# Moving work on VectorE's queue in a fused recurrence and gated-MLP kernel: C scaling earlier and chained, chunk 2's statistics in phase 0, norms one a group, two y slots within phase 3

## The chip, the cores and the metric

The kernel runs on one NeuronCore of a Trainium2 chip. The metric is the device time of one execution in microseconds (us). Most executions agree within about 1%. Each kernel was run several times beside the kernel before, on the same chip. "Span" is the length of the profiled execution as the profile sees it, some 2 us less than its time. The engines are PE (TensorE matmul; PEld in a page is its weight load), DVE (VectorE), ACT (ScalarE), POOL (GpSimd) and SP (here the queue that issues most DMAs).

## The reference, cut to what matters

```python
x = A_x                                   # 1 x 2048 x 448, bf16
xn = layernorm(x)
# A: a diagonal complex recurrence over the 2048 tokens
Lam_bar = exp(dt * (Lambda_re + 1j * Lambda_im))
B_bar = ((Lam_bar - 1) / Lam)[:, None] * (B_re + 1j * B_im)
h[t] = Lam_bar * h[t-1] + B_bar @ xn[t]
s = 2 * real(h @ C.T) + xn * Dskip
# B: a gated MLP, F = 1792
g = silu((sigmoid(xn @ w_gate) * (xn @ w_up)) @ w_down)
out = x + s * g
```

## The kernel before

The 2048 tokens are cut into four chunks of 512, and the program into four phases. In phase c, PE computes gate, up and B products of chunk c ("gu" banks), the down product of chunk c-1 ("acc") and y of chunk c-2 ("acc"). ACT evicts gu and computes sigmoids. DVE multiplies gate and up into hF, runs the recurrence (ta, tb, z, two scans "wv", then hT) and finishes the outputs. Before a chunk can be multiplied it is normalized: DVE takes its statistics, POOL a power, ACT writes xn, and a DMA transposes xn to xnT.

Every engine executes its own instructions in program order. A small planner at build time decides DVE's order: `side` is a queue of recurrence and similar steps, `late` holds evictions with an estimated time.

```python
def stat(g, t0, i, n):                    # one token tile of 128: mean and variance
    V.bn_stats(out=stats[:], in_=x_all[:, t0 + i, :])
    V.bn_aggr(out=mvs[g][:, i, :], in_=stats[:])
def stat_chain(g, t0, n, ...):            # -mean and, through POOL's power, 1/sd
    ...
    nc.gpsimd.tensor_tensor(out=sd_b, in0=ve_b, in1=half[:], op=ALU.pow)
    ...
def norm_slot(tt):                        # a tile of chunks 2 and 3
    xm = norm_a(tt, False); norm_b(tt, xm, False)    # ACT
    dup(tt)                               # POOL
    dma_transpose(tt)                     # SP queue

def c_steps():                            # C scaled by a per-state constant: 8 items
    def scaled(i): nc.scalar.activation(tmps[i][r, :], re, ACT.Copy, scale=...)   # ACT half
    def go(i): V.scalar_tensor_tensor(out=dst, in0=im, ..., in1=tmps[i][r, :], ...)  # DVE half -> cT
    ...
def ssm(c):                               # chunk c's recurrence into DVE's side queue
    ss = ssm_steps(c)                     # pair(0) + pair(1) + stack() + pair(2)
    if c == 0:                            # woven in, one after each step from the ninth on:
        ex = []
        for g in (2, 3):                  # statistics of chunks 2 and 3
            ex += [(0.7, lambda i=i, g=g: stat(g, 4 * g, i, 4)) for i in range(4)]
            ex.append((0.4, lambda g=g: stat_chain(g, 4 * g, 4)))
        ex.append((0.6, emit_diag))
        ss = weave(ss, ex + c_steps(), 8, 1)         # then the C items
    side.extend(ss)

def y_slot(c, j):                         # PE: xnT x diag(Dskip) + hT x cT
    ...
    for i, (hm, cm) in enumerate(K_ORDER):
        nc.tensor.matmul(y[:, cols], lhsT=hTs[c][:, hm, ...], rhs=K["cT"][:, cm, cols], ...)
# ... cut
run_phase(layout(2, "gbg gbg gbg gbg ggg ggg"), sides, norms(3, 0, 4))   # first y slots: chunk 0
ssm(3)
d, y = downs(2), ys(1)
sides = [[y[k], d[k]] for k in range(4)] + [[], []]
run_phase(layout(3, "gbg gbg gbg gbg ggg ggg"), sides)
for dur, fn in ys(2) + downs(3) + ys(3):
    plan.slot(dur, fn)
```

## Time and profile before

| | before |
|---|---|
| time, median of the first 3 runs | 205.41 us (205.40 to 206.59) |
| span of the profiled execution | 202.7 us |
| PE, DVE, ACT busy | 93%, 86%, 58% |
| PE idle for cT in the first y of chunk 0 | 3.8 us |

The page of the profile, parts 1, 2 and 4: busy time of each engine, then busy tenths of PE and DVE and the clock granted to PE in 40 slices of 5.07 us, and the shares of the chain of waits by engine.

```profile
PE 188.7 (93%) x1032; PEld 86.6 (43%) x1047; DVE 173.6 (86%) x385; ACT 116.6 (58%) x214; POOL 15.5 (8%) x38
...
PE   7999999899999999966999999999999999789983
...
DVE  7979895589999669963389999999999999999964
...
PEclk9999999999999999996999999999999999999999
...
DVE 47%; PE 6%; ACT 3%; issue 1%
```

PE is busy nearly everywhere from the second slice on. Two slices (86 to 96 us) read 6, and PEclk reads 6 in the second of them and 9 in its neighbours. The chain of work that ended last runs through DVE for 47% of the span.

What PE waited for (columns: engine, line, what the wait ended on; then us in total, times, longest):

```profile
PE acc L721 <- DVE cT L448: 3.8, 2, 2.4
PE acc L718 <- DVE g_t L725: 1.7, 2, 1.5
...
PE acc L721 <- DVE hT L632: 1.0, 1, 1.0
```

The timeline of PE at the first y (start, duration, engine, line, operation, out<-in, shapes, count; in brackets the idle time before it and its releaser):

```profile
87.77 0.36 PE L718 MATMUL acc<-diag,xnT 128*128 128x128 bf16 x4
87.97 1.11 PE L721 MATMUL acc<-cT,hT 128*128 128x448 bf16 x5
90.45 0.35 PE L721 MATMUL acc<-cT,hT 128*128 128x448 bf16 x1 [1.37 <-DVE cT L448]
93.22 0.53 PE L721 MATMUL acc<-cT,hT 128*128 128x448 bf16 x1 [2.42 <-DVE cT L448]
93.54 2.82 PE L697 MATMUL acc<-wd,hFa 128*128 128x448 bf16 x7
96.16 1.66 PE L697 MATMUL acc<-wd,hFb 128*128 128x448 bf16 x7
97.65 0.81 PE L470 MATMUL gu<-xnT,wg 128*128 128x512 bf16 x3
```

One y slot takes 1.52 us when nothing stops it, one down slot 2.65. Here y lasts from 87.77 to 93.54, and the down slot behind it from 93.54 to 97.65, because the clock fell. That is 9.88 us instead of 4.17.

The timeline of DVE: the first z of chunk 0, the first of chunk 2's statistics, the last hT of chunk 0, the last C item, and the first step of chunk 1's recurrence.

```profile
41.09 0.69 DVE L606 TENSOR_TENSOR z<-ta,tb 128x1024 bf16<-128x1024 bf16 x1
...
50.91 0.62 DVE L234 BATCH_NORM_STATS2 stats<-x_all 128x6 f32<-128x448 bf16 x1
...
86.55 0.72 DVE L632 TENSOR_TENSOR hT<-ta_1194,tb_1198 128x1024 bf16<-128x1024 bf16 x1
...
92.48 0.68 DVE L448 SCALAR_TENSOR_TENSOR cT<-cw,n2r,ctmp 64x448 bf16<-64x448 bf16 x1 [1.37 <-ACT ctmp L443]
...
99.16 0.69 DVE L592 TENSOR_TENSOR ta<-bus,cosT 128x1024 bf16<-128x1024 bf16 x1
```

### The profile page before, as it was taken

How to read it: one execution, taken by the hardware profiler on the slowest of the kernel's cores; microseconds unless marked ns; L12 is line 12 of the kernel's file. 1: busy time of each engine (PE TensorE's matmuls, PEld its weight loads, DVE VectorE, ACT ScalarE, POOL GpSimd, SP SyncE). 2: the span in 40 equal slices, each digit the busy share in tenths (PEclk: the TensorE clock that was granted, in tenths of full speed). 3: DMA queues.
4: the chain of work that ended last, by engine and by line, in shares of the span. 5: the costliest groups of instructions: out<-in, count | busy, mean ns of one | idle time of the engine just before them, and what ended most of it. 6: DMA issues, size and time to landing. Idle time of an engine off the chain costs nothing.

```text
span 202.7 us, 2922 instructions
## 1 busy us (share of the span) xinstructions
PE 188.7 (93%) x1032; PEld 86.6 (43%) x1047; DVE 173.6 (86%) x385; ACT 116.6 (58%) x214; POOL 15.5 (8%) x38
## 2 busy tenths in 40 slices
PE   7999999899999999966999999999999999789983
PEld 2564343244444443322454444354544443445542
DVE  7979895589999669963389999999999999999964
ACT  2539689895357999992375851654462836403300
POOL 4502302000030400000000000000000000000000
PEclk9999999999999999996999999999999999999999
DMA  5899998400000220011001010000000000011002
GB/s 165 267 326 156 261 358 173 82 0 0 0 0 3 52 52 0 2 29 49 0 0 49 27 26 23 0 0 26 0 24 0 26 23 0 0 49 45 0 23 70
DMA packets 23238, 12.08 MB, mean 60 GB/s; under 512 B 14772, under 2 KB 23224, under 8 KB 23224
## 3 DMA queue, kind: packets, MB, share of 16 engines
q1 hardware_dynamic: 22928, 11.73, 23.0%
q10 hardware_dynamic: 296, 0.18, 0.3%
q8 instruction: 8, 0.13, 0.3%
q14 instruction: 6, 0.05, 0.1%
HBM read 6.66 MB, written 1.84 MB: 42 GB/s over the span
## 4 chain that ended last, share of the span: by engine, by line
DVE 47%; PE 6%; ACT 3%; issue 1%
DVE wv L612 11%; DVE g_t L725 4%; DVE hT L632 3%; DVE z L606 3%; DVE x_all L726 3%; DVE tb L592 2%; DVE ta L592 2%; DVE hFb L520 2%; PE acc L697 2%; PE acc L721 2%; DVE hFa L520 2%; DVE g_t L705 2%; PE gu L470 1%; ACT ctmp L443 1%; ACT ub L514 1%
## 5 line engine op out<-in xcount | busy, mean ns | idle before, releaser
L470 PE MATMUL gu<-xnT,wg 128*128 128x512 bf16 (+1 forms) x168 | 44.8, 369 | 2.1 <-issue 1.1
L470 PE MATMUL gu<-xnT,wu 128*128 128x512 bf16 (+1 forms) x173 | 45.0, 368 | 0.4
L513 ACT ACTIVATE sig<-gu 128x512 bf16<-128x512 f32 x43 | 26.4, 614 | 22.3 <-PE gu L475 22.2
L700 ACT ACTIVATE sigd<-acc 128x448 bf16<-128x448 f32 x16 | 8.7, 542 | 38.9 <-PE acc L697 38.8
L721 PE MATMUL acc<-cT,hT 128*128 128x448 bf16 (+1 forms) x112 | 23.8, 348 | 4.8 <-DVE cT L448 3.8
L470 PEld LDWEIGHTS <-wg 128*128 128x128 bf16 x177 | 15.2, 97 | 25.4 <-issue 12.4
L514 ACT CAST ub<-gu 128x512 bf16<-128x512 f32 x43 | 25.8, 600 | 0.0
L470 PEld LDWEIGHTS <-wu 128*128 128x128 bf16 x177 | 17.3, 98 | 19.0
L697 PE MATMUL acc<-wd,hFa 128*128 128x448 bf16 x112 | 25.1, 366 | 0.1
L697 PE MATMUL acc<-wd,hFb 128*128 128x448 bf16 x112 | 24.0, 354 | 0.0
L475 PE MATMUL gu<-xnT,wk 64*128 64x512 bf16 (+1 forms) x118 | 18.9, 369 | 0.1
L697 PEld LDWEIGHTS <-hFa 128*128 128x128 bf16 x112 | 11.3, 100 | 13.9 <-issue 4.0
L470 PE MATMUL gu<-xnT,bT 128*128 128x512 bf16 x70 | 17.1, 379 | 0.0
L697 PEld LDWEIGHTS <-hFb 128*128 128x128 bf16 x112 | 11.1, 99 | 10.6 <-issue 0.7
L721 PEld LDWEIGHTS <-hT 128*128 128x128 bf16 x119 | 10.4, 98 | 9.7 <-issue 1.6
L552 ACT CAST bus<-gu 128x1024 bf16<-128x1024 f32 x12 | 12.4, 1030 | 0.8 <-PE gu L475 0.8
L520 DVE TENSOR_TENSOR hFb<-sig,ub 128x512 bf16<-128x512 bf16 x22 | 8.9, 417 | 3.5 <-ACT ub L514 3.5
L725 DVE TENSOR_TENSOR g_t<-acc,g_t 128x448 bf16<-128x448 f32 (+1 forms) x16 | 9.7, 603 | 2.1 <-PE acc L721 2.1
L520 DVE TENSOR_TENSOR hFa<-sig,ub 128x512 bf16<-128x512 bf16 x21 | 8.6, 412 | 3.1 <-ACT ub L514 3.1
L509 ACT ACTIVATE th<-gu 128x512 f32<-128x512 f32 x13 | 8.0, 614 | 5.1 <-PE gu L475 5.0
L470 PEld LDWEIGHTS <-bT 128*128 128x128 bf16 x72 | 7.0, 98 | 8.5
L475 PEld LDWEIGHTS <-wk 64*128 64x128 bf16 x118 | 5.0, 94 | 12.4 <-issue 9.7
(211 smaller groups left out, 270.7 us busy)
## 6 DMA issues: line engine op xcount, KB each, us to landing
out_dram<-x_all SPq DMA_DIRECT2D x15, 112.0 KB, 1.7
wd<-in_B_w_down_dram SPq DMA_DIRECT2D x1, 1568.0 KB, 9.0
wg<-in_B_w_gate_dram SPq DMA_DIRECT2D x2, 480.0 KB, 7.7
wu<-in_B_w_up_dram SPq DMA_DIRECT2D x2, 480.0 KB, 8.4
x_all<-in_A_x_dram SPq DMA_DIRECT2D x1, 896.0 KB, 5.4
x_all<-in_A_x_dram SPq DMA_DIRECT2D x1, 448.0 KB, 6.3
wg<-in_B_w_gate_dram SPq DMA_DIRECT2D x1, 384.0 KB, 4.3
wu<-in_B_w_up_dram SPq DMA_DIRECT2D x1, 384.0 KB, 4.1
```

The costliest lines, as they stand in the source:

```text
L470: nc.tensor.matmul(self.bank[:, i, cols], lhsT=get(kt), rhs=self.xnT[:, kt, cols], start=(kt == 0 and first), stop=(kt == KF - 1 and not f ...
L475: nc.tensor.matmul(self.bank[:, i, cols], lhsT=ap, rhs=self.xnT[r, 3, cols], start=first, stop=not first)
L513: nc.scalar.activation(th[:], gu[:, 0, :], ACT.Sigmoid)
L514: nc.scalar.copy(out=ub[:], in_=gu[:, 1, :])
L520: V.tensor_tensor(out=hF, in0=th[:], in1=ub[:], op=ALU.mult)
L552: nc.scalar.copy(out=bus[:], in_=bu[:])
L592: V.tensor_tensor(out=t[dst][:], in0=src, in1=tab, op=ALU.mult)
L612: V.tensor_tensor_scan(out=t["wv"][:, k, :], data0=rb, data1=t["z"][:, k, :], initial=(st[pt][:, k, :] if c else 0.0), op0=ALU.mult, op1=A ...
L697: nc.tensor.matmul(dacc[:, 0:D], lhsT=hF_at(c, ft)[:, j * P:(j + 1) * P], rhs=wd[:, ft, :], start=(ft == 0), stop=(ft == FT - 1))
L700: nc.scalar.activation(sigd[:], dacc[:, 0:D], ACT.Sigmoid)
L721: nc.tensor.matmul(y[:, cols], lhsT=hTs[c][:, hm, j * P:(j + 1) * P], rhs=K["cT"][:, cm, cols], start=False, stop=(i == 6))
L725: V.tensor_tensor(out=g_t[:, cols], in0=y[:, cols], in1=g_t[:, cols], op=ALU.mult)
```

## The change

Four edits move work; none removes or adds any. (1) The C items start right after the first pair of chunk 0's recurrence, and each item puts the next but one in motion, as "late" work, instead of standing in the weave. (2) Chunk 2's statistics leave the weave and go into phase 0. (3) `run_phase` gives out one norm a group instead of all that are ready. (4) Two of chunk 2's four y slots go between the last gate groups of phase 3.

```diff
@@ c_steps
-        steps = [(0.0, lambda i=i: scaled(i)) for i in range(2)]
-        for i in range(n):
-            if i + 2 < n:
-                steps.append((0.0, lambda i=i: scaled(i + 2)))
-            steps.append((0.6, lambda i=i: go(i), lambda i=i: scaled_at[i]))
-        return steps + [(0.0, lambda: h_done.add("c"))]
+        def step(i):
+            go(i)
+            if i + 2 < n:
+                start(i + 2)
+            if i == n - 1:
+                h_done.add("c")
+        def start(i):
+            scaled(i)
+            plan.add_late(scaled_at[i], 0.6, lambda: step(i))
+        return [(0.0, lambda: (start(0), start(1)))]
@@ phase 0, ahead of the edge constants
     side += [(0.7, lambda i=i: V_norm(4 + i), ...) for i in range(4)]
+    side += [(0.7, lambda i=i: stat(2, 8, i, 4)) for i in range(4)]
+    side.append((0.4, lambda: stat_chain(2, 8, 4)))
     side.append((0.0, constants))
@@ ssm
-            ex = []
-            for g in (2, 3):
-                ex += [(0.7, lambda i=i, g=g: stat(g, 4 * g, i, 4)) for i in range(4)]
-                ex.append((0.4, lambda g=g: stat_chain(g, 4 * g, 4)))
-            ex.append((0.6, emit_diag))
-            ss = weave(ss, ex + c_steps(), 8, 1)
+            ex = c_steps() + [(0.6, emit_diag)]
+            ex += [(0.7, lambda i=i: stat(3, 12, i, 4)) for i in range(4)]
+            ex.append((0.4, lambda: stat_chain(3, 12, 4)))
+            ss = weave(ss, ex, 8, 1)
@@ run_phase
-            while extras and extras[0][0] <= p and (p == len(groups) - 1 or ...):
+            last = p == len(groups) - 1
+            n = len(extras) if last else 1 + (bool(extras) and p > extras[0][0] + 1)
+            while n and extras and extras[0][0] <= p and (last or ...):
                 extras.pop(0)[1]()
+                n -= 1
@@ phase 3
-    sides = [[y[k], d[k]] for k in range(4)] + [[], []]
+    z = ys(2)
+    sides = [[y[k], d[k]] for k in range(4)] + [[z[0]], [z[1]]]
     run_phase(layout(3, "gbg gbg gbg gbg ggg ggg"), sides)
-    for dur, fn in ys(2) + downs(3) + ys(3):
+    for dur, fn in z[2:] + downs(3) + ys(3):
```

More of the change, by code (lines that the diff above doesn't have):

```diff
@@ L843, in run_phase @@
             group(units)
-            while extras and extras[0][0] <= p and (p == len(groups) - 1 or not extras[0][2] or extras[0][2]()):
+            last = p == len(groups) - 1
+            n = len(extras) if last else 1 + (bool(extras) and p > extras[0][0] + 1)
+            while n and extras and extras[0][0] <= p and (last or not extras[0][2] or extras[0][2]()):
                 extras.pop(0)[1]()
+                n -= 1
             for dur, fn in (sides[p] if sides else ()):
```

## The prediction

> **What bounds it now.** The span is 202.7 us; PE is busy 93% of it, DVE 86% (page, part 1). From 8 us on PE runs its stream back to back; time is lost where it stops. The inner stops (timeline and waits of PE): 0.94 us at 38.5 us; 1.37 and 2.42 us in the first y of chunk 0 (88 to 93 us), released by DVE writing cT; 1.49 and 0.21 us before y of chunk 2 (acc not freed by DVE's g_t); 1.00 us in y of chunk 3, for the last hT. The long stop also costs clock: from 91 to 96 us 0.6 is granted, and the next down slot takes 4.1 us instead of 2.65. The Trainium skill ("TensorE: Matmul & The Clock Gate", Part 1) says that about one idle window of 3.4 us halves the clock; the trace agrees: 3.8 us idle in two pieces, then starts 0.37 us apart instead of 0.19.
> From 94 us the chain of waits runs through DVE, filled to the end (52.1 of 53 us from 140 us): a backlog, since chunk 1's recurrence begins only at 99.2 us, behind C scaling, statistics and waits (2.34 us for rsd, 1.1 and 1.5 for ub, 1.4 for ctmp, 4.0 for g_t).
>
> **What the change does.** Work is only moved.
> - The eight C items (0.60 us each on DVE, 0.57 on ACT), now at 75 to 93 us, follow the first pair of chunk 0's recurrence, from about 50 us; cT should be complete by 65 us. C lies in memory by 36 us.
> - Chunk 2's statistics (3.1 us of DVE, at 51 to 57 us) go into phase 0, where DVE idles 1.3 + 1.2 + 2.2 us from 33 to 41 us; their x landed by 26 us. The edge constants slip; the first recurrence at most 1 us.
> - Norms one a group: ACT no longer holds four in a row (64.9 to 70.1 us), POOL's power for chunk 3's rsd isn't stuck behind four copies; the 2.34 us wait goes.
> - Two of chunk 2's y slots go between the last gate groups, so their evictions spread.
>
> **On the critical path.** Chunk 0's hT, finished at 87.3 us, should be done by 81 to 84 (3.1 us of statistics and 3 to 4 us of idle less, 1.8 us of C more). PE reaches y of chunk 0 at 87.8 us and won't stop: 3.8 + 1.45 us. DVE then runs over 10 us ahead; chunk 3 is held only by y of chunk 1, so its hT is ready: 1.0 us. Of the 1.7 us before y of chunk 2 I count 1.0. Sum 7.2 us, less 0.2 for new collisions: 7 us. PE's stream is the floor; over 8.5 us can't come out.
>
> **Prediction:** 198.4 us, 196.8 to 201.0. Faster by over 2%: 0.90, within 2%: 0.09, slower: 0.01.
>
> **What would show it.** Waits: no "PE acc <- DVE cT"; "acc <- DVE hT" under 0.3 us; "acc <- DVE g_t" under 1 us. Clock 0.9 or more in every slice from 10 us on. Timeline of DVE: cT written from 50 to 65 us; chunk 1's first ta before 86 us. The chain of waits mostly PE in the second half. DVE and ACT busy times change by under 2 us.
>
> **What would make it wrong.** Phase 0 slips: statistics delay the edge constants, tanh is kept longer (0.60 instead of 0.33 us on DVE an item), PE stops over 1 us around 39 us. ACT in phase 1, with norms and C halves, frees the gu banks late. DVE, gated by y of chunk 1, puts gate products behind a recurrence, so that PE waits for gu or hF. Then 201 us or more.

## The result, and the profile after

The changed kernel takes 196.99 us (median of 4 runs, 196.42 to 198.03), the kernel before beside it 205.91 us (4 runs). The ratio is 0.957, with a 95% interval from 0.9514 to 0.9627. Ratios here are the mean time of one kernel's fast runs over that of the other's fast runs of the same rounds, so not quite the ratio of the quoted medians. The results are correct.

The page after, the same parts:

```profile
PE 189.8 (97%) x1047; PEld 87.0 (44%) x1047; DVE 174.0 (89%) x385; ACT 116.4 (59%) x214; POOL 16.9 (9%) x38
...
PE   7999999998999999999999999999999999999992
...
DVE  7739989945999999999999999999999399999964
...
PEclk9999999999999999999999999999999999999998
...
PE 90%; ACT 3%; DMA 2%; issue 1%; DVE 1%; ACTq 1%; POOL 0%
```

PE reads 9 in every slice but one from the second to the last but one, the clock never falls before the end, and the chain that ended last is now PE for 90%. What PE waited for, all of it (the first is the warm-up at the start):

```profile
PE wps L222 <- POOL one L160: 1.3, 1, 1.3
PE gu L477 <- ACT ub L521: 0.8, 1, 0.8
PE gu L477 <- ACT ub L517: 0.2, 1, 0.2
PE gu L477 <- DVE xnT L293: 0.2, 1, 0.2
```

The three waits shown of before are gone. One of 0.84 us, for a gu bank at 46.75 us, is there instead. PE at the first y:

```profile
89.91 0.36 PE L725 MATMUL acc<-diag,xnT 128*128 128x128 bf16 x4
90.10 1.49 PE L728 MATMUL acc<-cT,hT 128*128 128x448 bf16 x7
91.43 1.49 PE L704 MATMUL acc<-wd,hFa 128*128 128x448 bf16 x7
92.75 1.49 PE L704 MATMUL acc<-wd,hFb 128*128 128x448 bf16 x7
94.08 0.81 PE L477 MATMUL gu<-xnT,wg 128*128 128x512 bf16 x3
```

The stretch that took 9.88 us takes 4.17. DVE after, the same instructions (the last hT of chunk 0 is at 87.69), and the last hT of chunk 3 (186.41).

```profile
35.31 0.62 DVE L234 BATCH_NORM_STATS2 stats<-x_all 128x6 f32<-128x448 bf16 x1
...
51.65 0.69 DVE L613 TENSOR_TENSOR z<-ta,tb 128x1024 bf16<-128x1024 bf16 x1
...
77.84 0.68 DVE L448 SCALAR_TENSOR_TENSOR cT<-cw,n2r,ctmp 64x448 bf16<-64x448 bf16 x1
...
87.69 0.69 DVE L639 TENSOR_TENSOR hT<-ta,tb 128x1024 bf16<-128x1024 bf16 x1
88.29 0.69 DVE L599 TENSOR_TENSOR ta<-bus,cosT 128x1024 bf16<-128x1024 bf16 x1
```
```profile
186.41 0.69 DVE L639 TENSOR_TENSOR hT<-ta,tb 128x1024 bf16<-128x1024 bf16 x1
```

**Start and body.** The start differs from run to run: the first gate matmul begins at 8.37 us in the profiled execution before and at 10.98 us in the one after, which was the slowest of its four. The columns after must be read 2.6 us earlier when they are compared. I call "body" the span minus the start of the first gate matmul. It is a steadier measure of one trace than the span: 194.33 us before and 185.02 after. A second profile of the changed kernel (after_again, below) gave 185.46. Cut at the same places of PE's stream:

| stretch of PE's stream | before, us | after, us | gained |
|---|---|---|---|
| first gate matmul to the first of phase 1 | 31.03 | 30.02 | 1.01 |
| to the first y of chunk 0 | 48.37 | 48.91 | -0.54 |
| that y and the down slot behind it | 9.88 | 4.17 | 5.71 |
| to the first y of chunk 3 | 94.07 | 92.07 | 2.00 |
| to the very last y part | 6.52 | 5.40 | 1.12 |
| to the end | 4.46 | 4.45 | 0.01 |
| body | 194.33 | 185.02 | 9.31 |

The first two rows differ between executions of one kernel: in after_again they are 31.48 and 47.90 us (PE stops there 1.38 us ahead of phase 1, and not later), together 0.02 us less than before. The three rows below them repeat; they sum up to 8.83 us.

### The profile page after: what moved, and what is told of

It reads as the page before. It is cut to its first block, busy times and chain, and to the rows that moved or that the text cites. A ratio compares the mean times of both kernels' runs of the same rounds, so it can differ in the third digit from the quotient of the medians.

```text
span 196.0 us, 2932 instructions
## 1 busy us (share of the span) xinstructions
PE 189.8 (97%) x1047; PEld 87.0 (44%) x1047; DVE 174.0 (89%) x385; ACT 116.4 (59%) x214; POOL 16.9 (9%) x38
## 4 chain that ended last, share of the span: by engine, by line
PE 90%; ACT 3%; DMA 2%; issue 1%; DVE 1%; ACTq 1%; POOL 0%
PE gu L477 45%; PE acc L704 22%; PE acc L728 10%; PE gu L482 9%; PE wps L222 2%; DMA vrow<-in_A_Lambda_im_dram 2%; PE acc L725 2%; ACT L520 1%; DVE g_t L732 1%; ACT th L516 1%; PE tpx L288 1%; ACT ub L517 1%; DVE x_all L733 0%; PE tpx L290 0%; ACTq L208 0%
## 5 line engine op out<-in xcount | busy, mean ns | idle before, releaser
L477 PE MATMUL gu<-xnT,wg 128*128 128x512 bf16 (+1 forms) x177 | 46.2, 370 | 1.2 <-ACT ub L521 0.8
L477 PE MATMUL gu<-xnT,wu 128*128 128x512 bf16 (+1 forms) x177 | 45.9, 368 | 0.0
L520 ACT ACTIVATE sig<-gu 128x512 bf16<-128x512 f32 x42 | 25.8, 614 | 22.5 <-PE gu L482 22.4
L521 ACT CAST ub<-gu 128x512 bf16<-128x512 f32 x42 | 25.2, 600 | 0.0
L704 PE MATMUL acc<-wd,hFa 128*128 128x448 bf16 x112 | 23.8, 352 | 0.0
L728 PE MATMUL acc<-cT,hT 128*128 128x448 bf16 (+1 forms) x112 | 23.2, 347 | 0.0
L619 DVE TENSOR_TENSOR_SCAN wv<-r_col,st,z 128x512 bf16<-128x512 f32 x18 | 22.6, 1276 | 0.2
L282 POOL COPY xn<-xn 128x64 bf16<-128x64 bf16 x12 | 6.5, 538 | 73.4 <-ACT xn L278 63.3
L516 ACT ACTIVATE th<-gu 128x512 f32<-128x512 f32 x14 | 8.6, 614 | 5.1 <-PE gu L482 5.0
```

The costliest lines, as they stand in the source:

```text
L477: nc.tensor.matmul(self.bank[:, i, cols], lhsT=get(kt), rhs=self.xnT[:, kt, cols], start=(kt == 0 and first), stop=(kt == KF - 1 and not f ...
L516: nc.scalar.activation(th[:], gu[:, 0, :], ACT.Tanh, scale=0.5)
L520: nc.scalar.activation(th[:], gu[:, 0, :], ACT.Sigmoid)
L521: nc.scalar.copy(out=ub[:], in_=gu[:, 1, :])
L619: V.tensor_tensor_scan(out=t["wv"][:, k, :], data0=rb, data1=t["z"][:, k, :], initial=(st[pt][:, k, :] if c else 0.0), op0=ALU.mult, op1=A ...
L704: nc.tensor.matmul(dacc[:, 0:D], lhsT=hF_at(c, ft)[:, j * P:(j + 1) * P], rhs=wd[:, ft, :], start=(ft == 0), stop=(ft == FT - 1))
```

## The experiments

**Theory.** PE's stream is the floor, and the change is worth exactly the stops that it takes out of this stream. **Rivals.** DVE's backlog is the bound (the chain before says so), so what counts is the DVE time moved. And, as to the four parts: each pays its own share, or only some of them matter.

| kernel | median, us | ratio to before, 95% | body, us |
|---|---|---|---|
| changed kernel | 196.99 | 0.957 (0.9514 to 0.9627) | 185.02 |
| c_alone: before + part 1 | 201.24 | 0.973 (0.9641 to 0.982) | 188.45 |
| stats_alone: before + part 2 | 197.27 | 0.9583 (0.9519 to 0.9647) | 185.19 |
| no_c: changed - part 1 | 196.80 | 0.956 (0.949 to 0.9631) | 185.03 |
| no_stats: changed - part 2 | 205.94 | 1.0009 (0.9955 to 1.0064) | 194.59 |
| no_norms: changed - part 3 | 196.70 | 0.9556 (0.9511 to 0.9602) | 185.38 |
| no_y: changed - part 4 | 196.16 | 0.9552 (0.9489 to 0.9614) | 185.18 |
| warm_fill: before, PE kept warm | 204.40 | 0.9935 (0.9853 to 1.0016) | 192.70 |
| dve_load_2: changed + DVE work | 196.94 | 0.9578 (0.9503 to 0.9653) | 185.43 |
| dve_load_3: changed + DVE work later | 199.12 | 0.9657 (0.9586 to 0.9727) | no usable trace |
| after_again | 197.54 | 0.9575 (0.9531 to 0.9619) | 185.46 |
| start_order | 196.73 | 0.9534 (0.948 to 0.9588) | 185.34 |
| start_edges | 196.96 | 0.9572 (0.9527 to 0.9617) | 186.14 |

One run each of c_alone, dve_load_3 (1,093.79 us, see below) and start_order was slow and is in the median, not in the ratio.

### c_alone: the C items early and chained, nothing else

```diff
# on the kernel before, with the new c_steps
-            ss = weave(ss, ex + c_steps(), 8, 1)
+            ss = weave(ss, c_steps() + ex, 8, 1)
```

> The kernel before with one part of the change: the eight C items start, chained, right after the first pair of chunk 0's recurrence; statistics, norms and y slots stay. Theory (PE's own stream is the floor, and the change is worth what it takes out of PE's stops): the stop in the first y of chunk 0 shrinks from 3.8 us to what chunk 0's last hT leaves, which DVE now finishes at about 88 to 89 us, so at most 1.2 us, and the clock does not fall; DVE starts chunk 1 ten microseconds earlier, so the stops in the last two y groups go as well. Gain 5 to 7.5 us of the 8.9. Rival (DVE's backlog is the bound, so each part counts by the DVE time it moves): C alone moves nothing out of DVE's total, and gains under 3 us.

It gained 5.88 us of body, some 60% of the whole, within the 5 to 7.5 us that were expected, but not in the way expected. The waits for cT, g_t and hT are all gone, and a new one stands first in the list of PE's waits:

```profile
PE gu L477 <- DMA xnT<-xn: 3.0, 1, 3.0
```

In its timeline the stop lies at the start of phase 2; it ends 9.5 us ahead of the y that the change was meant to speed up (92.95 us):

```profile
83.46 0.81 PE L477 MATMUL gu<-xnT,wg 128*128 128x512 bf16 x3 [3.02 <-DMA xnT<-xn]
```

The C items, put first, pushed chunk 2's statistics back. The step that closes them (ve_b) is written at 65.21 us here and at 57.39 before. ACT then begins chunk 2's norms at 75.13 us instead of 64.94 (first line: before; second: c_alone; c_alone started 2.4 us later, so the true delays are 5.4 and 7.8 us):

```profile
64.94 0.71 ACT L270 ACTIVATE xm<-x_all,nmean 128x448 bf16<-128x448 bf16 x1
...
75.13 0.67 ACT L270 ACTIVATE xm<-x_all,nmean 128x448 bf16<-128x448 bf16 x1
```

The transposed chunk lands when PE has been waiting for 3.0 us. So one stop was traded for another, shorter one. The prediction had not seen that the two jobs compete for the same places in DVE's queue.

### stats_alone: chunk 2's statistics in phase 0, nothing else

```diff
# on the kernel before
     side += [(0.7, lambda i=i: V_norm(4 + i), ...) for i in range(4)]
+    side += [(0.7, lambda i=i: stat(2, 8, i, 4)) for i in range(4)]
+    side.append((0.4, lambda: stat_chain(2, 8, 4)))
@@ ssm
-            for g in (2, 3):
+            for g in (3,):
```

> The kernel before with one part of the change: chunk 2's statistics in phase 0. Theory: the C steps, still woven in their old order, come about 3 to 5 us earlier, and so does chunk 0's last hT; cT is complete at about 88 us instead of 93, the stop of PE there falls to under 1 us and the clock holds; gain 4 to 6 us. Rival (only the early, chained C items take the stop away): gain under 2 us.

It gained more than either theory expected: as much as the whole change, 197.27 us, and a body of 185.19 us. In DVE's timeline the last C item starts at 85.55 us, and PE reaches the first y at 88.04 us:

```profile
85.55 0.68 DVE L448 SCALAR_TENSOR_TENSOR cT<-cw,n2r,ctmp 64x448 bf16<-64x448 bf16 x1
```
```profile
88.04 0.36 PE L718 MATMUL acc<-diag,xnT 128*128 128x128 bf16 x4
88.24 1.49 PE L721 MATMUL acc<-cT,hT 128*128 128x448 bf16 x7
```

The C items, in their old form and order, are in time by more than a microsecond, because the five statistics steps ahead of them are gone. The first C item starts at 68.83 us, or 68.1 with the later start taken off, instead of 75.33. That is more than the 3.1 us of work that left, since the weave puts a step of the recurrence beside each of the five, and the 2.34 us wait for rsd lay among them. And the norms of chunk 2 are in time, because their statistics were taken before.

### no_stats: everything but the statistics

```diff
# on the changed kernel
-    side += [(0.7, lambda i=i: stat(2, 8, i, 4)) for i in range(4)]
-    side.append((0.4, lambda: stat_chain(2, 8, 4)))
@@ ssm
             ex = c_steps() + [(0.6, emit_diag)]
-            ex += [(0.7, lambda i=i: stat(3, 12, i, 4)) for i in range(4)]
-            ex.append((0.4, lambda: stat_chain(3, 12, 4)))
+            for g in (2, 3):
+                ex += [(0.7, lambda i=i, g=g: stat(g, 4 * g, i, 4)) for i in range(4)]
+                ex.append((0.4, lambda g=g: stat_chain(g, 4 * g, 4)))
```

> The changed kernel with chunk 2's statistics back in the weave, behind the C items; C early, norms one a group and y slots stay as changed. Theory (the statistics' early place is what takes PE's stops away, since it serves both cT and chunk 2's norms): like c_alone, PE waits about 3 us for chunk 2's xnT at the start of phase 2, with a clock that may fall; 199 to 202 us, 2.5 to 5 us more than the changed kernel. Rival (with norms and y slots added, C early suffices): within 1 us of the changed kernel.

It lost more than expected: all of the gain. PE's stop before phase 2 and the page's clock:

```profile
PE gu L477 <- DMA xnT<-xn: 7.3, 1, 7.3
```
```profile
87.72 1.44 PE L477 MATMUL gu<-xnT,wg 128*128 128x512 bf16 x3 [7.32 <-DMA xnT<-xn]
88.95 1.49 PE L477 MATMUL gu<-xnT,wu 128*128 128x512 bf16 x3
```
```profile
PEclk9999999999999999759999999999999999999999
```

With late statistics, one norm a group is harmful: ACT makes two of chunk 2's norms by 77.7 us and the other two only from 81.47, after the next group's evictions. In c_alone, where all four go out at once, the fourth is done at 80.3. The stop grows from 3.0 to 7.3 us, and then the clock falls: three gate matmuls take 1.44 us instead of 0.81. That part 3 does this is read from the traces; no run has part 1 and part 3 alone.

### no_c, no_norms, no_y: the other three parts, each left out

```diff
# no_c: the changed kernel with the old c_steps, behind statistics and diagonal
-            ex = c_steps() + [(0.6, emit_diag)]
-            ex += [(0.7, lambda i=i: stat(3, 12, i, 4)) for i in range(4)]
-            ex.append((0.4, lambda: stat_chain(3, 12, 4)))
-            ss = weave(ss, ex, 8, 1)
+            ex = [(0.7, lambda i=i: stat(3, 12, i, 4)) for i in range(4)]
+            ex += [(0.4, lambda: stat_chain(3, 12, 4)), (0.6, emit_diag)]
+            ss = weave(ss, ex + c_steps(), 8, 1)
# no_norms: the old while loop in run_phase
# no_y: sides = ... + [[], []], and ys(2) + downs(3) + ys(3) at the end
```

> The changed kernel with the C items in their old form (16 steps in the weave, each waiting for its ACT half) behind chunk 3's statistics and the diagonal. Theory: only that cT is complete before PE reaches y of chunk 0 at 88 us counts. The statistics that went to phase 0 let the C steps come five places earlier, so cT is complete by about 85 us and the result is within 1 us of the changed kernel. If instead the early place or the chaining counts by itself, it loses 3 us or more, with PE waiting for cT again.

> The changed kernel with the old loop, which gives out all norms that are ready at once. Since chunk 2's statistics are now done in phase 0, all four norms of chunk 2 would go by their places (0, 0, 1, 2, 3 of the spread) and not pile up much. Theory: PE has no stop there either way, so within 0.5 us of the changed kernel.

> The changed kernel with all four y slots of chunk 2 behind phase 3, as before. Theory: PE runs into four y slots back to back with two acc buffers, DVE is busy with chunk 3, and PE waits 1 to 1.7 us for acc; the time grows by 1 to 2 us. Rival (with C early DVE is ahead anyway, so those waits go by themselves): under 0.4 us.

All three are the same as the changed kernel: bodies of 185.03, 185.38 and 185.18 us. For no_c this is what the theory said: its last C item starts at 85.01 us, and PE starts y at 87.50. For no_y the rival was right, and my theory was not. All four y slots of chunk 2 run there back to back without a stop (they begin 1.52 us apart), since DVE, which is ahead of PE by then, frees the accumulators in time:

```profile
167.25 0.36 PE L725 MATMUL acc<-diag,xnT 128*128 128x128 bf16 x4
...
168.77 0.36 PE L725 MATMUL acc<-diag,xnT 128*128 128x128 bf16 x4
...
170.29 0.36 PE L725 MATMUL acc<-diag,xnT 128*128 128x128 bf16 x4
...
171.81 0.36 PE L725 MATMUL acc<-diag,xnT 128*128 128x128 bf16 x4
```

Together with stats_alone and no_stats this settles what is needed: part 2 is sufficient, and without it the other three together bring nothing. It does not give each part a share: part 1 alone brings 5.88 us of body, because parts 1 and 2 take away the same stop.

### warm_fill: the stop stays, the idleness goes

```diff
# on the kernel before, in y_slot, ahead of the first accumulation
+            if (c, j) == (0, 0):
+                for _ in range(16):
+                    nc.tensor.matmul(y[:, 0:D], lhsT=ident[:, :], rhs=wd[:, 0, :], start=True, stop=True)
```

> The kernel before, with 16 extra 128x448 matmuls into the accumulator just ahead of the first y of chunk 0 (about 3.0 us of PE work inside the 3.8 us stop; the accumulation starts after them, so the result is unchanged). It leaves the wait for cT as it is and takes only the idleness away. Theory (the stop costs 1.45 us more by the clock): no slice with a granted clock of 0.6, the down slot after it takes 2.65 instead of 4.1 us, and the time falls by 1 to 1.5 us although PE does more work. Rival (the slow down slot has another cause, or PE regains it later because DVE is the bound): within 0.4 us.

```profile
88.09 3.19 PE L719 MATMUL acc<-wd,ident 128*128 128x448 bf16 x16
...
93.53 0.35 PE L724 MATMUL acc<-cT,hT 128*128 128x448 bf16 x1 [0.92 <-DVE cT L448]
93.72 1.49 PE L697 MATMUL acc<-wd,hFa 128*128 128x448 bf16 x7
95.04 1.49 PE L697 MATMUL acc<-wd,hFb 128*128 128x448 bf16 x7
96.37 0.81 PE L470 MATMUL gu<-xnT,wg 128*128 128x512 bf16 x3
```

PE now works through the stop (16 useless matmuls, from 88.09 until y's own begin at 91.12) and still waits 0.92 us for the last C item, but the down slot behind takes 2.65 us (93.72 to 96.37) and the page shows a clock of 9 in every slice but the last. The body is 1.6 us shorter than before. By time the ratio of 0.9935 is 1.3 us less, with an interval that includes 1, so the time alone doesn't decide; the trace shows the mechanism. The granted clock agrees in all four executions: 0.997 to 1.0, where the kernel before has 0.983 to 0.992.

### dve_load_2 and dve_load_3: useless DVE work, early and late

```diff
# on the changed kernel, x only for c == 2 (dve_load_2) or c == 3 (dve_load_3)
+    def idle_work():
+        V.bn_stats(out=dmy[:], in_=wd[:, 0, :])
-        return pair(0) + pair(1) + stack() + pair(2)
+        x = [(0.0, idle_work)] if c == 3 else []
+        return x + pair(0) + x + pair(1) + x + stack() + x + pair(2)
```

> The changed kernel with four useless statistics instructions on DVE (0.6 us each, 2.4 us in sum), one ahead of each part of chunk 2's recurrence. Theory: DVE is ahead of the gate of chunk 3 (y of chunk 1) by the 3.2 us that it idles at 151 to 155 us, so they vanish there: under 0.4 us. Rival (DVE's total is the bound): 2 us or more.

> The changed kernel with the same four instructions, one ahead of each part of chunk 3's recurrence, behind the gate. In the trace chunk 3's last hT is written 187.1 us, 0.07 us later than PE wants it. Both theories: the time grows by about 2.0 to 2.5 us; with dve_load_2 unchanged this shows that DVE bounds the last stage alone.

2.4 us more DVE work in chunk 2 change nothing (196.92 us mean of its fast runs); in the trace DVE's two waits at 151 to 155 us shrink from 3.2 to 1.2 us. The same work in chunk 3 costs 1.85 us (198.77 us mean of its three fast runs, on the same chip), a little under the expected 2.0 to 2.5. With three and four fast runs the intervals of the two ratios still overlap, and the costlier one has no usable trace, so this second half is likely rather than shown. So DVE's total is not the bound after the change, although DVE is busy 89% of the span; it seems to bound only the last stage, where chunk 3's recurrence cannot begin before y of chunk 1 has freed its hT buffer and must end when PE gets to y of chunk 3. In the profiled execution of the changed kernel the last hT starts at 186.41 us and PE enters that y at 186.15; it lost 0.07 us there.

The profiled execution of dve_load_3 took 1,093.79 us, so its trace can't be compared. In it PE's 128x448 matmuls of y took 1,593 ns each (median) where they otherwise take 353, while DVE and ACT took their usual time; the recorded clock was 1.0. The cause stays open; none of the other 86 timed executions showed it.

### after_again, start_order and start_edges: looking for a better version

Two weak places were left: the start, 8.4 to 11 us until the first gate matmul, and the stop of 0.4 to 1.4 us around the start of phase 1. In the profiled execution of the changed kernel the chain goes in the start through the landing of the small vectors (1.7% of the span), and PE and DVE stand behind it in program order.

```diff
# start_order, on the changed kernel
-    emit_warm(8)
-    emit_columns()
-    emit_warm(N_WARM - 8)
+    emit_warm(N_WARM + 2)
...  # vsb copy and emit_theta go behind the second statistics, nu_1(0) ahead of nu_2(0)
-        emit_warm(1 + j)
+        emit_columns() if j else emit_warm(1)
# start_edges: besides, in phase 0
+    side.append((0.0, constants))
     side += [(0.7, lambda i=i: stat(2, 8, i, 4)) for i in range(4)]
     side.append((0.4, lambda: stat_chain(2, 8, 4)))
-    side.append((0.0, constants))
```

> The changed kernel once more, on the chip of the next two runs, to compare them with: 196 to 198 us. The scatter is in the start: the first gate matmul comes at 8.4 to 11 us, depending on when the small vectors land; from there to the end 185.0 us, within 0.3.

> The changed kernel with the matmuls that turn the four small vectors into columns moved on PE from ahead of the first transposes to behind them, and on DVE the copy of the columns and the first table step likewise. Theory (in slow starts PE and DVE stand, in order, behind the landing of the vectors, and the clock then falls): the first gate matmul comes at about 8.4 us in each run, the scatter between runs falls under 1 us, the median falls by 0.5 to 1.5 us. Rival (what comes late in slow starts is x itself, or the start isn't on the path): no difference beyond 0.4 us.

> start_order, and in phase 0 the edge constants ahead of chunk 2's statistics instead of behind them. Theory: chunk 0's first z, which the change put off by 8 us, comes about 4 us or more earlier, the ACT table load falls into phase 0, and PE's stop at the start of phase 1 (0.4 to 1.3 us) becomes under 0.5 us; up to 0.6 us less than start_order. Rival (chunk 0's recurrence isn't on the path as long as its last hT comes before PE's first y): the earlier z buys nothing, within 0.3 us of start_order.

after_again is within its expected 196 to 198 us; its body of 185.46 is just outside the 185.0 within 0.3. start_order is not clearly better than after_again: 196.73 against 197.54 us, ratios of 0.9534 and 0.9575 with overlapping intervals. My expectation missed. The vectors no longer hold anything, but the first gate matmul comes at 9.26 us, not at 8.4: the chain's new link is PE's own warm-up. Sixteen warm-up matmuls end later than the norm that they wait for, since they started 0.43 us apart, instead of 0.21, for longer: up to 6.4 us here, up to 5.5 in start_edges (the first norm was ready at 6.2 us, and PE turned to it at 7.41). Fewer of them might bring the gain.

start_edges puts the edge constants back ahead of the statistics. Chunk 0's first z comes 1.6 us earlier (48.34 instead of 49.93 us in start_order; 1.1 us with the start taken off), not the 4 us expected. The stop near the start of phase 1 is 0.56 and 0.28 us instead of 1.27, but chunk 2's norms are again later, and a wait of 0.88 us for xnT comes back at 79 us. The body is 0.8 us longer than start_order's. So no version tried beats the changed kernel clearly; stats_alone equals it with the fewest edits.

## Why the prediction was right or wrong, point by point

- **The total was right, and the gain too small.** 198.4 us was predicted, from 196.8 to 201.0; 196.99 was measured, a gain of 8.9 us instead of 7.0. It was inside the range by luck: 0.2 us from its edge, with two of the four executions below it. "Over 8.5 us can't come out" was wrong: the body gained 9.31 us. That limit was a sum of the waits that the profile lists, and the list leaves things out.
- **"PE won't stop: 3.8 + 1.45 us."** The stretch gained 5.71. The stop and the slow down slot were as read; another 0.46 us went inside the y slot around the two waits, in no list. warm_fill confirms the clock's part with its own trace.
- **"Of the 1.7 us before y of chunk 2 I count 1.0"; "1.0 us" for chunk 3's hT.** They gained 2.00 and 1.12. The mis-sized term is the first: both stops went wholly, and 0.3 us of smaller gaps besides. The reason given, that two y slots between gate groups spread the evictions, was wrong: no_y keeps the gain without them.
- **The cause of the main gain was given to the wrong part.** The prediction let the C items' early place do it, and had the statistics help by 3.1 us. c_alone shows that early C alone trades the stop for one of 3.02 us for xnT, and stats_alone that the old C items are in time once the statistics are out of their way. The step that failed is "The eight C items ... follow the first pair": I followed what C gains and not what the statistics, pushed back, then delay. cT was also complete only at about 76 us (78.5 less the 2.6 us of start), not by 65.
- **"Norms one a group; the 2.34 us wait goes."** That wait is gone, but no_norms shows that the part is worth nothing here, and no_stats that it harms when statistics are late.
- **"The first recurrence at most 1 us" later was wrong.** Chunk 0's first z starts at 51.65, less 2.6, so 8 us later than before (41.09): the edge constants went on ACT behind three copies of B products, and the coefficients went ahead of z. Of chunk 0's recurrence only the last hT is near the path, so the delay cost at most the 0.84 us stop at 46.75 us, behind ACT's table load (44.33). The stop that the prediction feared, over 1 us around 39 us, did come in after_again (1.38 us at 40.62), without undoing the gain. That last hT came 1.5 us earlier than before (88.4 less 2.6 against 87.2 us), not at 81 to 84. The margin to PE's y is 1.5 us, where I believed it to be 4 to 7.
- **The signs in the profile.** No wait for cT, hT or g_t on PE; a clock of 9 in all slices but the last, which reads 8; the chain mostly PE; DVE and ACT busy within 0.5 us of before; as predicted but for that slice. Chunk 1's first ta comes at 88.29, less 2.6: 85.7 us, just before the 86 that was predicted.
- **The rival, DVE's backlog, falls for the changed kernel** by dve_load_2. For the kernel before it was half true: the chain of waits ran through a full DVE, but, as I read it (no run tests this order of cause), it was full because PE's stop had let the work pile up behind it; stats_alone, with the same DVE work, is 4% faster.

## What to carry to other kernels

When two jobs on one in-order engine each have their own deadline on another engine, moving one ahead of the other can trade one stop for another, as in c_alone; look for a third place, where the engine idles, for one of them. Cost a reordering by what gets pushed back as well as by what comes forward, and trace each pushed item to its last consumer. When a change has several parts, run each alone and each left out before crediting any: here one part of four is enough for the whole gain, and another alone brings some 60% of it.

## What the Trainium skill lacked or had wrong

- "TensorE: Matmul & The Clock Gate", Part 1, says that the clock halves after about one idle window of 3.4 us and recovers after a busy one. The runs agree: a stop of 7.32 us was followed by matmuls at about half speed for some 4 us (no_stats, 87.7 to 91.6), and one of 3.02 us by none in the profiled run (c_alone; two of its other three executions have a mean clock of 0.991, as the kernel before has, so the clock may have fallen there). For idleness in pieces the page tells of frequent small gaps without their length; here 1.37 and 2.42 us with a single matmul between them were enough (kernel before).
- The same page reports the gate stuck at a quarter for over 50 us, and records that can't be trusted. One execution here took 1,093.79 us, with matmuls of 1,593 ns instead of 353 and a recorded clock of 1.0. Seven matmuls of one y slot started in 7.88 us (477.45 to 485.33), 1.13 us apart instead of 0.19: a sixth of the usual rate, not a quarter. Whether it is the same thing no run shows.
- "ScalarE: Activation LUTs", What ACT_TABLE_LOAD costs, gives 1,283 ns and a drain of about 1,380 ns. The trace after has the load at 1.28 us (44.33 to 45.61), between an activation that ended at 44.31 and one that began at 45.62: no drain of that size stood around it.
